# Block loads on one or two DMA queues, and the order of small steps on GpSimd, in a bucketed attention and channel-mix kernel

## The chip, the cores and the metric

The kernel runs on one core of a Trainium2 chip. The metric is the device time of one execution in microseconds; the time of a kernel is the median over its runs. The engines are named as in the profile: PE (TensorE matmuls), PEld (its weight loads), DVE (VectorE), ACT (ScalarE), POOL (GpSimd) and SP (SyncE). SP, ACT and POOL also issue DMAs; a name with a q (SPq, ACTq) is such an engine's sequencer.

## The reference

Two layers in sequence. The first is attention with a mask by hash bucket (B = 4, H = 8, S = 768, D = 64; q, k, v in float32):

```python
q_bits = (np.einsum('bhsd,dk->bhsk', q, proj) > 0)      # proj: 64 x 6
k_bits = (np.einsum('bhsd,dk->bhsk', k, proj) > 0)
q_bucket, k_bucket = sum(bits * 2 ** arange(6))         # 64 buckets
scores = (q @ k.T) / 8, -1e9 where the buckets differ
attn = softmax(scores) @ v                              # denominator + 1e-9
```

Its output, 8 heads of 64 side by side, is x (4 x 768 x 512) of an RWKV channel mix:

```python
xk = mu_k * x + (1 - mu_k) * x_prev                     # x_prev: x shifted by one token
xr = mu_r * x + (1 - mu_r) * x_prev
k = np.maximum(xk @ w_k, 0)                             # w_k: 512 x 1024
out = sigmoid(xr @ w_r) * ((k * k) @ w_v)               # w_r: 512 x 512, w_v: 1024 x 512
```

## The kernel before

**Pairs and slots.** The 32 heads are worked on as 16 pairs, four pairs to a batch. A pair has 12 slots, for two heads of six chunks of 128 keys. The main loop runs over the slots G of all pairs; n is the pair and s the slot in it. `score` (L444, L451) issues two matmuls of 70 contraction rows and one exponential on ACT, which writes the tile pt. The 70 rows are 64 of the head and 6 bucket bits, as plus and minus a half: the bias and the scale of the exponential make the scores of unequal buckets vanish. `pv` (L462, L471) follows two slots later with the product with v; the denominator is a column of ones in va. After a pair `turn_out` (L496 to L502) transposes its output into xt, and shifts columns into a copy of the last token of the block before (a memset and a copy, L501 and L502; on GpSimd except for the last pair of a batch).

**How a pair gets ready.** Pairs 0 to 2 come by `load_qk` and are transposed on PE. Pairs from 3 on come by `load_blocks`: eight DMAs of 176 KB (side q or k, head j, half h), each of which writes 32 partitions from 32 * (2j + h). All eight are on SP. `turn_blocks` transposes 32 x 32 blocks on DVE (tq and tk, L347) and casts them on GpSimd into the rows aq and ak (L357, L359). `bits_blocks` multiplies with the projection on PE (bb, L373), one slot later takes the signs on DVE (sg, L383), and sends them by eight SP DMAs of 4.5 KB into rows 64 to 69 of aq and ak (L388). For pairs 1 and 2 that is `bits` (L401, L405, L411). All this runs ahead: in pair n, `load_blocks(n + 3)` and `load_v(n + 2)` are called at slot 1 (5 in pair 0, 3 in pair 1), `turn_blocks(n + 2)` at slots 7 and 8 of pairs 1 to 3 (6 and 7 in the first pair of a batch from pair 4 on, 4 and 5 in the others), and `bits_blocks(n + 2)` at slot 11 (10 from pair 4 on). blk has two buffers, vf three, and the sets of aq, ak and va are three.

**Values.** `values(n, j)` makes the bfloat16 tile va of head j and the sum vs of its rows on GpSimd (L428, L432 to L434) from vf.

**FFN.** From slot 5 of pair 4 on a queue of FFN items of the batch before is worked off between the slots, so many as a credit per slot allows: kp = xk w_k (L546, relu on ACT L569 or DVE L571, square on DVE L579), rp = xr w_r (tanh on ACT L588), vp = k2 w_v (os on DVE L611, stored by SP L615). The weights come by DMAs of GpSimd in the slots that the table `weights` gives.

**The order** on every engine is that of the program, written out by hand. `later(k, fn)` puts a function off to the start of a slot: `run_due()` runs, at the start of slot G, everything whose time is up, so that k = 0 and k = 1 within a slot both mean the next slot.

Of the kernel before, what the change touches and what calls it, by code (L numbers as in the profile page):

```python
# [31 lines left out]
def kernel(  # L32
# [13 lines left out]
    nc = tc.nc  # L46
# [8 lines left out]
    NPB = H // 2  # L55
    NPAIRS = B * NPB
# [121 lines left out]
    def fast():  # L178
        with ExitStack() as fx:
# [29 lines left out]
            for s in range(NSET):  # L209
                d = {}  # L210
# [6 lines left out]
            for s in range(NSET):  # L217
                d = []
# [16 lines left out]
            def later(k, fn):  # L235
                due.append((clock[0] + k, len(due), fn))

            def run_due():
                ready = sorted(x[:2] for x in due if x[0] <= clock[0])
                for key in ready:  # L240
                    fn = next(x for x in due if x[:2] == key)
                    due.remove(fn)
                    fn[2]()
# [19 lines left out]
                        )  # L263

            NTOK = S // 32

            def load_blocks(n):


                b, t = divmod(n, NPB)  # L270
                xb = blkp.tile([P, 2, NTOK, D], FP32, name=f"blk{n}", tag="blk")
                blks[n] = xb
                run = NC_ * D - 32
                for side, i, src in SIDES:
                    for j in range(2):
                        rows = src[b, 2 * t + j].rearrange("(w i c) d -> i w (c d)", w=4, i=32)
                        for h in range(2):
                            r0 = 32 * (2 * j + h)
                            nc.sync.dma_start(  # L279
                                out=xb[r0 : r0 + 32, i].rearrange("p (w c) d -> p w (c d)", w=4)[  # L280
                                    :, :, 0:run
                                ],
                                in_=rows[:, :, 32 * h : 32 * h + run],
                            )

            def load_v(n):
                b, t = divmod(n, NPB)
                vf = vfp.tile([P, 2, S // 2], FP32, name=f"vf{n}", tag="vf")
                nc.sync.dma_start(
                    out=vf, in_=v[b, 2 * t : 2 * t + 2].rearrange("j (p c) d -> p j (c d)", c=NC_)  # L290
                )
                vfs[n] = vf


            def norm(n, i):
# [8 lines left out]
                else:  # L304

                    nc.scalar.activation(
                        junk.rearrange("p (u d) -> p u d", u=NTOK),
                        blks[n][:, i, :, 0:32],
# [107 lines left out]
            def values(n, j):  # L416
                vf = vfs[n][:, j, :]
                va, vs = vsets[n % NSET][j]
                if n < NSET:
                    nc.gpsimd.memset(va[:, :, D : D + 1], 1.0)  # L420
                    nc.gpsimd.memset(vs[:, D : D + 1], float(NC_))
                if n < NKEEP:
                    nc.gpsimd.tensor_copy(
                        va[:, :, 0:D].rearrange("p (e c) d -> p e c d", e=2),
                        vf.rearrange("p (c e d) -> p e c d", e=2, d=D),
                    )
                else:
                    nc.gpsimd.tensor_copy(  # L428
                        va[:, :, 0:D], vf.rearrange("p (c d) -> p c d", d=D)
                    )  # L430
                s3 = sgp.tile([P, 3 * D], FP32, name=f"s3{n}_{j}", tag="s3")
                nc.gpsimd.tensor_add(s3, vf[:, 0 : 3 * D], vf[:, 3 * D : 6 * D])  # L432
                nc.gpsimd.tensor_add(s3[:, 0:D], s3[:, 0:D], s3[:, D : 2 * D])
                nc.gpsimd.tensor_add(vs[:, 0:D], s3[:, 0:D], s3[:, 2 * D : 3 * D])  # L434
                vas[n, j], vss[n, j] = va, vs
# [223 lines left out]
            def load_w(which, c0, nch):  # L659
                dst, src = {"k": (wk_sb, moe_w_k), "r": (wr_sb, moe_w_r), "v": (wv_sb, moe_w_v)}[  # L660
                    which
                ]
                nc.gpsimd.dma_start(
                    out=dst[:, c0 : c0 + nch, :],
                    in_=src[c0 * P : (c0 + nch) * P, :].rearrange("(c p) f -> p c f", p=P),
                )
# [11 lines left out]
            for _ in range(22):  # L678
# [6 lines left out]
            turn(0, 1, 1, "D")  # L685
            bits(0, (1,), "C")
            load_v(1)
            nc.sync.dma_start(
                out=mu_rows[0:NDC, :], in_=moe_mu_k.rearrange("(c p) -> c p", p=P)
            )  # L690
            nc.sync.dma_start(
                out=mu_rows[NDC : 2 * NDC, :], in_=moe_mu_r.rearrange("(c p) -> c p", p=P)
# [9 lines left out]
                0: {2: ("k", 0, 2)},  # L702
                2: {0: ("k", 2, 2)},
                3: {4: ("r", 0, 2), 8: ("r", 2, 2)},
                4: {11: ("v", 0, 4)},
                5: {10: ("v", 4, 4)},
            }
            LAG = 2
            MIXSLOT = 6
# [11 lines left out]
            for G in range(nslots + LAG):  # L721
                clock[0] = G
                n, s = divmod(G, 12)
                live = G < nslots
                run_due()

                if live and s == (5 if n == 0 else 3 if n == 1 else 1):
                    if n + 2 < NPAIRS:
                        load_v(n + 2)
                    if n + 3 < NPAIRS:  # L730
                        load_blocks(n + 3)
                w = weights.get(n, {}).get(s)
                if w:
                    load_w(*w)
                old = chunks[G - LAG] if G >= LAG else None
                first = old is not None and old[2] == 0
                if live:
                    score(*chunks[G])
                if old and not first:
                    pv(*old, oo_bank(*old[:2]))  # L740
                rate = 25.9 / (NPB * 12 + (3 if n >= NPAIRS - NPB else 0))
                ffn(rate / 2)
                mb = misc_bank(n, s)
                if live:
                    if n == 0:
                        if s in (0, 1):
                            turn(1, s, 1, "BD"[s])
                    if n == 1 and s == 0:
                        mups = bank(mb, [P, 2 * NDC], FP32, "mups")
                        nc.tensor.transpose(mups, mu_rows, ident32[0 : 2 * NDC, 0 : 2 * NDC])  # L750
                        nc.vector.tensor_copy(mu_sb, mups)
                    if s == (3 if n == 0 else 1) and n + 1 < NKEEP:
                        bits(n + 1, (0, 1), mb)
                    if s == (11 if n < NPB else 10) and NKEEP <= n + 2 < NPAIRS:
                        bits_blocks(n + 2, mb if n < NPB else "A")
                    if s == 3 and n >= 1:
                        turn_out(n - 1, mb)
                    if n >= NPB:
                        if s == 4 and n % NPB == 0:
                            mix((n - 1) // NPB, (n - 1) % NPB, 0)  # L760

                        if s in (8, 9) and n % NPB:
                            mix((n - 1) // NPB, (n - 1) % NPB, 0, [(0,), (1, 2)][s - 8])
                    ms = (5, 6, 11)
                    if s in ms and 1 <= n < NPB:
                        mix(0, n - 1, 0, [ms.index(s)])

                    xs = [NPB * 12 + x for x in (5, 10, 11, 12)]
                    if G in xs:
                        mix(0, xs.index(G), 1)  # L770
                    if n > NPB and s == (10 if n % NPB else 5):
                        mix((n - 1) // NPB, (n - 1) % NPB, 1)
                    if s in (5, 7, 9, 11) and n + 2 < NKEEP:
                        x = (s - 5) // 2
                        turn(n + 2, x % 2, x // 2, mb)
                    ts = (7, 8) if n < NPB else (6, 7) if n % NPB == 0 else (4, 5)
                    if s in ts and NKEEP <= n + 2 < NPAIRS:
                        turn_blocks(n + 2, ts.index(s))
                    vs_ = (6, 10) if n == 0 else (0, 2)
                    if s in vs_ and n + 1 < NPAIRS:  # L780
                        values(n + 1, vs_.index(s))
                    if s - 2 in ts and NKEEP <= n + 2 < NKEEP + NLARGE:
                        largest(n + 2, ts.index(s - 2))
                    if s in (8, 10) and NKEEP + NLARGE <= n + 2 < NPAIRS:
                        norm(n + 2, (s - 8) // 2)
                ffn(rate / 2)
                if old and first:
                    pv(*old, oo_bank(*old[:2]))
                if live and n >= NPB and n % NPB == 0 and s == MIXSLOT - 1:
                    queue.extend(ffn_items(n // NPB - 1))  # L790
# [218 lines left out]
```

## Time and profile before

| | us |
|---|---|
| median of 3 runs | 275.18 (274.89 to 275.69) |
| the profiled execution | 277.73 |
| its span | 275.9 |
| PE busy | 250.1 (91%) |
| ACT busy | 210.3 (76%) |
| DVE busy | 179.7 (65%) |
| POOL busy | 123.3 (45%) |
| mean granted PE clock | 0.971 of full speed |

The page gives the busy time of each engine over the span, then the span in 40 slices of 6.9 us (a digit is the busy share in tenths), the DMA queues, the chain of work that ended last, and the costliest groups of instructions. The trace also answers for a stretch of time: rows of an engine's instructions with the idle time before each group in brackets, waits, the chain of waits, and windows. Start times are microseconds from the start of the span. The SP queue's 24,744 packets carry 32.32 MB; the DMAs of GpSimd carry 4.19 MB.

### The profile page before, as it was taken

Reading aid. Unit: us, or ns where it says so; the run is one execution under the profiler, and the core shown is the slowest. Engines: PE = TensorE matmul, PEld = TensorE weight load, DVE = VectorE, ACT = ScalarE, POOL = GpSimd, SP = SyncE. Lnnn points to the kernel's source line nnn. Section 1 sums busy time; section 2 is a strip of 40 time slices with the busy share of each in tenths; the row PEclk is TensorE's granted clock in tenths of the full one; section 3 lists DMA queues with packets and bytes.
Section 4 is the critical chain, followed back from the end, with each engine's and each line's share of the span. In section 5 each row is a group of like instructions: output and inputs, shape, how many; then the busy total and the mean of one; then the engine's idle time right before and its main releaser. Section 6 shows DMA issues by size and latency. Waiting matters only on the chain.

```text
span 275.9 us, 6536 instructions
## 1 busy us (share of the span) xinstructions
PE 250.1 (91%) x2377; PEld 149.1 (54%) x2407; DVE 179.7 (65%) x369; ACT 210.3 (76%) x306; POOL 123.3 (45%) x246
## 2 busy tenths in 40 slices
PE   7899786989995999999999999998999999899970
PEld 5466452656552564656565656564656665455440
DVE  3765546497876676677779696758596646776340
ACT  2199785699995999797999998988999988086100
POOL 5886593667674355550748093815583000000000
PEclk9999999599997999999999999999999999999995
DMA  7457695979594947393949091968720002220140
GB/s 249 155 115 180 125 227 125 240 156 222 128 222 128 217 118 161 103 239 106 246 150 209 7 234 39 216 172 208 181 62 7 2 2 76 78 76 0 46 169 30
DMA packets 27769, 37.42 MB, mean 136 GB/s; under 512 B 3400, under 2 KB 23952, under 8 KB 27728
## 3 DMA queue, kind: packets, MB, share of 16 engines
q1 hardware_dynamic: 24744, 32.32, 46.4%
q0 software_dynamic: 2592, 4.19, 7.6%
q8 instruction: 21, 0.34, 0.5%
q10 hardware_dynamic: 392, 0.40, 0.4%
q14 instruction: 20, 0.16, 0.2%
HBM read 32.64 MB, written 6.29 MB: 141 GB/s over the span
## 4 chain that ended last, share of the span: by engine, by line
PE 57%; DMA 18%; ACT 8%; SPq 6%; DVE 5%; issue 3%; POOL 0%; ACTq 0%; DVEq 0%; POOLq 0%
PE sc L444 14%; PE vp L546 13%; PE kp L546 10%; DMA blk<-in_k_dram 8%; PE oo L471 7%; ACT pt L451 6%; PE rp L546 5%; DMA vf<-in_v_dram 5%; PE bb L373 3%; SPq L279 2%; SPq L411 2%; PE ot L496 2%; DMA blk<-in_q_dram 1%; PE oo L462 1%; DMA aq<-sg 1%
## 5 line engine op out<-in xcount | busy, mean ns | idle before, releaser
L451 ACT ACTIVATE pt<-sc,expb 128x768 bf16<-128x768 f32 x192 | 166.5, 910 | 33.5 <-PE sc L444 31.2
L444 PE MATMUL sc<-aq,ak 70*128 70x384 bf16 x384 | 96.4, 332 | 4.3 <-ACT pt L451 1.1
L471 PEld LDWEIGHTS <-pt 128*128 128x128 bf16 x1152 | 61.9, 99 | 28.2 <-issue 2.5
L471 PE MATMUL oo<-va,pt 128*128 128x65 bf16 x1152 | 67.7, 195 | 0.0
L546 PE MATMUL kp<-xk,wk_sb 128*128 128x384 bf16 x256 | 55.7, 325 | 2.6 <-DVE kr L571 1.1
L444 PEld LDWEIGHTS <-ak 70*128 70x128 bf16 x384 | 35.1, 99 | 34.6 <-issue 12.7
L546 PE MATMUL vp<-wv_sb,k 128*128 128x512 bf16 (+1 forms) x188 | 48.8, 370 | 0.4
L357 POOL CAST aq<-tq 64x768 bf16<-64x768 f32 x26 | 21.4, 823 | 33.3 <-DVE tq L347 21.1
L579 DVE TENSOR_TENSOR k<-kr 128x384 bf16<-128x384 bf16 x64 | 27.3, 442 | 3.4 <-ACT kr L569 3.0
L546 PEld LDWEIGHTS <-wk_sb 128*128 128x128 bf16 x256 | 21.7, 97 | 14.1 <-issue 4.0
L546 PE MATMUL rp<-wr_sb,xr 128*128 128x512 bf16 x78 | 25.4, 391 | 3.5 <-DVE kr L571 2.8
L359 POOL TENSOR_SCALAR ak<-tk 64x768 bf16<-64x768 f32 x26 | 22.3, 857 | 8.5 <-DVE tk L347 6.7
L569 ACT ACTIVATE kr<-kp 128x384 bf16<-128x384 f32 x36 | 18.1, 502 | 9.3 <-PE kp L546 9.2
L546 PEld LDWEIGHTS <-k 128*128 128x128 bf16 x200 | 16.9, 97 | 12.8 <-issue 2.5
L611 DVE SCALAR_TENSOR_TENSOR os<-th,vp 128x512 f32<-128x512 bf16 (+1 forms) x25 | 16.5, 662 | 9.6 <-PE vp L546 7.5
L502 POOL COPY xt<-xt 128x127 bf16<-128x127 bf16 x12 | 3.5, 294 | 42.8 <-DVE xt L497 42.8
L432 POOL TENSOR_TENSOR s<-vf 128x192 f32<-128x192 f32 x32 | 21.3, 665 | 0.0
L571 DVE TENSOR_SCALAR kr<-kp 128x384 bf16<-128x384 f32 x28 | 15.4, 550 | 8.4 <-PE kp L546 8.2
L497 DVE COPY xt<-ot 128x768 bf16<-128x768 bf16 x16 | 8.9, 556 | 18.2 <-PE ot L496 18.2
L482 DVE RECIPROCAL rc<-oo 128x6 f32<-128x6 f32 x32 | 6.1, 191 | 21.6 <-PE oo L471 21.6
L428 POOL CAST va<-vf 128x384 bf16<-128x384 f32 x26 | 15.1, 582 | 8.0 <-DMA vf<-in_v_dram 7.6
L483 DVE TENSOR_TENSOR ob<-oo,rc 128x384 bf16<-128x384 f32 x32 | 17.8, 557 | 1.1
(79 smaller groups left out, 279.8 us busy)
## 6 DMA issues: line engine op xcount, KB each, us to landing
blk<-in_q_dram SPq DMA_DIRECT2D x52, 176.0 KB
blk<-in_k_dram SPq DMA_DIRECT2D x52, 176.0 KB
vf<-in_v_dram SPq DMA_DIRECT2D x16, 384.0 KB
out_dram<-os SPq DMA_DIRECT2D x23, 256.0 KB
aq<-sg SPq DMA_DIRECT2D x64, 4.5 KB
wk_sb<-in_moe_w_k_dram POOLq DMA_DIRECT2D x2, 512.0 KB, 7.3
wv_sb<-in_moe_w_v_dram POOLq DMA_DIRECT2D x2, 512.0 KB, 10.4
ak<-sg SPq DMA_DIRECT2D x62, 4.5 KB
```

What stands on the lines that cost most here:

```text
L357: eng.tensor_copy(dst, src)
L359: eng.tensor_scalar(out=dst, in0=src, scalar1=ALPHA, scalar2=1.0, op0=ALU.mult, op1=ALU.mult,)
L432: nc.gpsimd.tensor_add(s3, vf[:, 0 : 3 * D], vf[:, 3 * D : 6 * D])
L444: nc.tensor.matmul(sc[:, sp, 0:HALF], au["k", j][:, jc * P : (jc + 1) * P], au["q", j][:, sp * HALF : (sp + 1) * HALF], start=True, stop=True,
L451: nc.scalar.activation(pt.rearrange("p (s q) -> p s q", s=2), sc[:, :, 0:HALF], AF.Exp, bias=expb, scale=SCALE,)
L471: nc.tensor.matmul(oo[:, ic, :], pts[n, j, jc][:, ic * P : (ic + 1) * P], vas[n, j][:, jc, :], start=False, stop=(jc == NC_ - 1 and ic == ...
L483: nc.vector.tensor_tensor(out=obs[n][:, :, j * D : (j + 1) * D], in0=oo[:, :, 0:D], in1=rc.to_broadcast([P, NC_, D]), op=ALU.mult,)
L546: nc.tensor.matmul(box["t"], lhs(), rhs(), start=(i == 0), stop=(i == len(mms) - 1))
L569: nc.scalar.activation(kr, kp, AF.Relu, scale=HALFROOT)
L571: nc.vector.tensor_scalar(out=kr, in0=kp, scalar1=0.0, scalar2=HALFROOT, op0=ALU.max, op1=ALU.mult,)
L579: lambda: nc.vector.tensor_tensor(out=k2, in0=kr, in1=kr, op=ALU.mult),
L611: nc.vector.scalar_tensor_tensor(out=os_, in0=mx["th", b, c][:, ms], scalar=1.0, in1=vp, op0=ALU.add, op1=ALU.mult,)
```

## The change

It has four parts.

1. `load_blocks` for pairs 3 to 8 (NTWO = 9): the loads of head j = 0, partitions 0 to 63, are issued on SP at once, those of j = 1, partitions 64 to 127, on ACT's queue, by `later(0)` to `later(3)`: two at the start of the next slot and one at the start of each of the two slots after. The order of the loops over h and j is exchanged, for pairs from 9 on too, which stay on SP.
2. `load_v(2)` is issued in the preamble, after `load_v(1)` and ahead of the mu rows; in the loop `load_v(n + 2)` begins with pair 1.
3. The first half of w_v is loaded from slot 2 of pair 5 rather than slot 11 of pair 4.
4. In pairs before the fifth, `values(n + 1, 0)` is called at slot 4 (6 in pair 0, as before) and `values(n, 1)` at slot 0 of its own pair; from the fifth pair on `values(n + 1, j)` stand at slots 0 and 2 as before, with `values(4, 1)` at slot 0 of pair 4. In pairs 1 to 3 the shift of columns in `turn_out` (slot 3) thus precedes `values(n + 1, ·)` on GpSimd.

```diff
+            NTWO = 9
...
+                k = 0
                 for side, i, src in SIDES:
-                    for j in range(2):
-                        rows = src[b, 2 * t + j].rearrange("(w i c) d -> i w (c d)", w=4, i=32)
-                        for h in range(2):
+                    for h in range(2):
+                        for j in range(2):
+                            rows = src[b, 2 * t + j].rearrange("(w i c) d -> i w (c d)", w=4, i=32)
                             r0 = 32 * (2 * j + h)
-                            nc.sync.dma_start(
-                                out=xb[r0 : r0 + 32, i].rearrange("p (w c) d -> p w (c d)", w=4)[
-                                    :, :, 0:run
-                                ],
-                                in_=rows[:, :, 32 * h : 32 * h + run],
-                            )
+
+                            def load(eng, r0=r0, i=i, h=h, rows=rows):
+                                eng.dma_start(
+                                    out=xb[r0 : r0 + 32, i].rearrange(
+                                        "p (w c) d -> p w (c d)", w=4
+                                    )[:, :, 0:run],
+                                    in_=rows[:, :, 32 * h : 32 * h + run],
+                                )
+
+                            if j and n < NTWO:
+                                later(k, lambda load=load: load(nc.scalar))
+                                k += 1
+                            else:
+                                load(nc.sync)
...
             load_v(1)
+            load_v(2)
...
-                4: {11: ("v", 0, 4)},
-                5: {10: ("v", 4, 4)},
+                5: {2: ("v", 0, 4), 10: ("v", 4, 4)},
...
-                    if n + 2 < NPAIRS:
+                    if 1 <= n < NPAIRS - 2:
                         load_v(n + 2)
...
-                    vs_ = (6, 10) if n == 0 else (0, 2)
-                    if s in vs_ and n + 1 < NPAIRS:
-                        values(n + 1, vs_.index(s))
+                    if n < NPB:
+                        if s == (6 if n == 0 else 4):
+                            values(n + 1, 0)
+                        if n and s == 0:
+                            values(n, 1)
+                    else:
+                        if s == 0 and n == NPB:
+                            values(n, 1)
+                        if s in (0, 2) and n + 1 < NPAIRS:
+                            values(n + 1, s // 2)
```

## The prediction

> **What bounds the kernel now.** I read the page's 40 slices first. TensorE (PE) is full except in slices 5, 7 and 13, each 6.9 us long, and ScalarE (ACT) has its holes in the same places:
>
> ```profile
> PE   7899786989995999999999999998999999899970
> ACT  2199785699995999797999998988999988086100
> ```
>
> The first pairs, to about 61 us, are a stage without FFN work, in which ACT's exponentials set the pace: 12 slots of 0.79 us, 9.5 us for a pair. From slot 5 of pair 4 on PE is the bound, since FFN matmuls fill what the scores leave. So I look for what stopped both, in ACT's own rows (start, duration, engine and line, operation, and in brackets the idle time before and who ended it):
>
> ```profile
> 16.37 8.22 ACT L451 ACTIVATE pt<-sc,expb 128x768 bf16<-128x768 f32 x10 [0.43 <-PE sc L444]
> 25.07 8.02 ACT L451 ACTIVATE pt<-sc,expb 128x768 bf16<-128x768 f32 x10 [0.47 <-PE sc L444]
> 35.36 9.61 ACT L451 ACTIVATE pt<-sc,expb 128x768 bf16<-128x768 f32 x12 [2.27 <-PE sc L444]
> 49.07 2.84 ACT L451 ACTIVATE pt<-sc,expb 128x768 bf16<-128x768 f32 x3 [4.10 <-PE sc L444]
> 87.18 0.90 ACT L451 ACTIVATE pt<-sc,expb 128x768 bf16<-128x768 f32 x1 [3.26 <-PE sc L444]
> ```
>
> Three stalls: 2.27 before 35.36, 4.10 before 49.07, 3.26 before 87.18. What lies in front of them the chain of waits says (start, duration, what):
>
> ```profile
> 26.10 6.61 DMA blk<-in_k_dram
> 36.83 5.83 DMA blk<-in_k_dram
> 42.68 3.68 DMA ak<-sg
> 46.36 0.97 DVE tk L347
> 75.13 9.13 DMA blk<-in_k_dram
> 84.39 0.98 DVE tk L347
> ```
>
> All three are block loads that land late and hold the DVE transpose. The windows of 3.41 us (window, length, busy time of PE, PEld, DVE, ACT, POOL, then granted PE clock, DMA share, GB/s) show the second price, the clock afterwards:
>
> ```profile
> 44.75:48.16 3.41, 1.03 (x8) 0.17 (x8) 1.82 (x3) 0.22 (x1) 1.87 (x3) 0.99 0.07 18
> 48.16:51.57 3.41, 3.41 (x29) 2.16 (x27) 2.61 (x5) 2.36 (x3) 1.24 (x3) 0.50 0.93 248
> 82.26:85.67 3.41, 0.79 (x10) 0.44 (x9) 1.28 (x2) 1.56 (x3) 0.50 (x2) 1.00 0.09 18
> ```
>
> The clock is 0.50 from 48.16 to 54.98 and from 85.67 to 89.08. Five exponentials from 49.07 need 4.84 to 53.91 instead of four times 0.79 = 3.16: 1.7 us lost to each such stretch. Pairs take (from first exponential to first exponential) 10.2, 12.5, 13.7, 11.9, 13.7 and 19.1 us for pairs 0 to 5, 14.0 to 14.7 after that.
>
> **The change part by part.** *Half of the blocks to ACT's queue.* SP loses 24 issues of 0.43 to 0.46 us; ACT's sequencer gains 24. Bandwidth is no gain: the loads of one pair land one each 0.83 us (26.93, 27.79, 28.61 and so on), 176 KB in 0.83 us or 212 GB/s at a DMA share over 1, while vf, with 128 partitions, runs at 345 to 409 GB/s. Whether halves on two queues go side by side or in turn no row shows: between nothing (8 x 0.83 = 6.6 us for a pair) and half (3.3 us). I take nothing; either way the data would then land 4 us or more before its transposes.
>
> The Trainium skill, "DMA: Bandwidth & Descriptors", section "Rules for kernel authors", speaks against it: spreading over issuing engines brings no bandwidth, and two transfers to disjoint halves of the partitions serialize; only issue time is saved. "SBUF — State Buffer", section "Can I just issue two DMAs to hit both halves?", gives +6% for two at once. By that figure a pair's load would be 6.3 us, an estimate; the sum stays as it is.
>
> The gain is that ACT's half no longer stands behind SP's eight small DMAs of the bucket bits (0.66 to 0.70 us each). They and the blocks hold each other up in the queue; SP's waits (who waited, for whom, total us, times, longest) say so:
>
> ```profile
> SPq L388 <- DMA blk<-in_q_dram: 6.1, 13, 1.2
> SPq L388 <- DMA blk<-in_k_dram: 5.3, 7, 2.3
> ```
>
> In pair 4 the eight bits issue from 63.68 to 71.20 and the blocks of pair 7 start only at 71.75, ten us behind their slot.
>
> The price is new waits on ACT. In the program as built every DMA of SP and ACT waits on one of eight counters, shared by both queues, until the DMA before it on that counter has landed. For the new ACT loads these are, in pair 0, a mu row and bits 3 and 6 of pair 1; in pairs 1 to 5 the 1st, 4th and 6th bits DMA of the pair two on, issued in the same pair. Behind a waiting load stand ACT's exponentials, and PE waits for those (two score tiles).
>
> *Pair 0.* Bits 1 to 8 issue on SP from 16.55 at 0.70; the first landed in 1.8 us (18.35), the third and sixth only at 22.26 and 22.84, for GpSimd's first half of w_k (issued 16.80, landed 22.1) was in the way. So the exponential of slot 8 starts not at 19.57 but after 22.84, two issues of 0.45 and a semaphore: 23.9. That is +4.3. Without the hold, bit 6 would land at 16.55 + 5 x 0.70 + 1.8 = 21.9 and slot 8 start at 22.4: +2.8. I take 4.3, since GpSimd's order there does not change.
>
> *Pairs 1 to 3.* With t the first exponential of the pair, sg (the bits) is ready at t + 0.8 (36.55 against 35.36, 50.0 against 49.07), bit 6 issues 5 x 0.70 later, lands 1.8 later and the load issues: t + 6.6. It stands ahead of the exponential of slot 4, and eight are left: 6.6 + 8 x 0.79 = 12.9. In pair 1 sg comes at t + 2.3 and the load stands ahead of slot 6: 8.15 + 6 x 0.79 = 12.9. Against 12.5, 13.7 and 11.9 that is +0.4, -0.8, +1.0. The old stalls at 35 and 49 are in the old periods, so they are gained and paid back here.
>
> *Pair 4.* Slot 4 moves from t + 3.2 (64.15) to t + 6.6: 3.4 later, and the FFN starts after it. PE had holes here and may catch up a part; between 0 and 3.4, taken 2.5, as the matmuls freed are few before slot 5.
>
> *Pair 5.* It is 4.7 us over its neighbours' mean (19.1 against 14.4): the stall at 83 to 86 and a half-clock window. ACT's half of the pair's blocks now issues near its slot, SP's half is four issues rather than eight, and the 4.7 go; late next are the load's own issues on ACT and its waits, under PE's work, 0.5. Net -4.2.
>
> *Clock.* Each stop of ACT for 2.5 to 3.4 us leaves PE two slots of work and then nothing. A PE hole of 2.4 us cost the clock in one place (44.97 to 47.37), and PE busy for 2.35 of 3.40 at 31.10 did not. For five such stops I take one half-clock stretch more than now and a little, 2.0; bounds 0 and four stretches, 6.8.
>
> *The rest, priced at nothing.* vf of pair 2 goes out 8 us earlier, SP's 0.45 us falling in its idle 15.52 to 16.55; uncovered, its 384 KB would hold the first bits DMA by 1.0. wv's first half issues 3 slots later, at about 77 instead of 73.08, landing by 87 to 91; its first matmul is at 105.9, so 15 us cover it. On GpSimd a half of the values is 0.58 + 0.67 + 2 x 0.32 = 1.9 us; the shift of columns (0.10 + 0.29) now goes ahead of it. The second half at slot 0 of its own pair is read first in slot 8, 6 us on; if GpSimd were behind by more, up to 1.9 per pair. GpSimd is busy 45% of the span, so nothing.
>
> **Sum.** 4.3 + 0.4 - 0.8 + 1.0 + 2.5 - 4.2 + 2.0 = +5.2 us. The profiled execution took 277.73 (span 275.9), 2.5 over the median of 275.18; I add the difference to the median: 280.4.
>
> **The rivals.** *Faster: ACT hardly waits.* If the bits have landed by the time ACT gets to its loads, under one exponential (0.8 us) of wait a pair, the stalls are gained: 2.3 + 4.1 + 1.7 + 4.7 = 12.8. Paid are 2.8 in pair 0 and 0.3 in each of pairs 1 to 4 (two issues in one slot, 0.9 against 0.79), 4.0. Since bits and casts still have to pass, I count 10 of the 12.8: -6, 269. For it: bits on an idle queue take 1.8 us, and SP is no longer held by blocks. Against: five issues at 0.70 before the sixth bit, which no faster transfer shortens. It decides at a wait of about 0.8 us a pair.
>
> *Even.* If pair 0 costs 2.8, PE catches up all of pair 4, and no clock window is added, the sum is 5.2 - 1.5 - 2.5 - 2.0 = -0.8: 274.4.
>
> *Slower still: every stop costs the clock.* Four stretches of 1.7, in place of 2.0, make 285.2. For it: the stops are as long as the two that did so. Against: the 31.10 window.
>
> *It does nothing.* If both queues drained as one and ACT's loads were late anyway, the three stalls would stand: 275.2. Against it: ACT's waits come from the program.
>
> **How the numbers follow.** Forecast 0.42, faster rival 0.22, even 0.14, slower still 0.20, nothing 0.02. Below 268.5 lies a third of the faster case, above 286 a third of the slower still: 0.14 outside. A measurement of this kernel tells 0.3%, 0.8 us, from no change. Even gives 0.05 faster, 0.05 same and 0.04 slower; so faster is 0.22 + 0.05 = 0.27, same 0.05 + 0.02 = 0.07, slower 0.42 + 0.20 + 0.04 = 0.66. As both signs hold much, the likeliest case by itself: 277 to 284.
>
> **What would show it.** Right: in ACT's rows a gap of 3 to 4 us near 20 us, ended by ACT's own queue with a wait for aq or ak from sg, and gaps of 2 to 3 us near slot 4 of pairs 2 to 4; first exponentials of pairs 1 to 4 12.9 apart; no hole in PE near 83. Wrong: pairs 1 to 4 at 10 to 11 us with ACT's loads issued between exponentials without idle time (the faster rival); a pair 5 still at 19 us (then the wv load, not SP's queue, held the blocks); or clock 0.50 in more than two stretches (the slower one).

## The result, and the profile after

The changed kernel took 299.17 us (median of 295.76, 299.10, 299.24 and one execution of 1385 us, which is left out of all ratios here and below, as slow executions are) against 275.44 for the kernel before, measured with it: a ratio of 1.0821, 95% interval 1.0728 to 1.0914. The profiled execution took 299.24, span 297.4. The direction was as forecast, the size was not: +24 us where +5 was expected, and above the range. Pairs 6 to 14 take 128.4 us in both profiled executions, and what follows them was 2.2 us shorter in the changed kernel's; the loss is in pairs 0 to 5:

| from first exponential to first exponential, us | pair 0 | 1 | 2 | 3 | 4 | 5 | sum |
|---|---|---|---|---|---|---|---|
| before | 10.2 | 12.5 | 13.7 | 11.9 | 13.7 | 19.1 | 81.1 |
| forecast, without its 2.0 for the clock | 14.5 | 12.9 | 12.9 | 12.9 | 16.2 | 14.9 | 84.3 |
| after | 16.9 | 17.4 | 16.9 | 15.4 | 17.3 | 20.8 | 104.7 |

The page's slices of the span (297.4 us, 7.4 us a slice) have more holes than before, and the clock (third row) is low from slice 4 to slice 12 without a break, and again in slice 15:

```profile
PE   7877967895969599999999999999899999989991
ACT  1246573876759469998989999988899998629400
PEclk9985677568779969999999999999999999999997
```

ACT's waits (who waited, for whom, total us, times, longest) name the new cause. In the kernel before ACT waited for no DMA:

```profile
ACT pt L462 <- DMA ak<-sg: 14.0, 5, 3.8
...
ACT pt L462 <- DMA blk<-in_q_dram: 3.3, 1, 3.3
...
ACT pt L462 <- DMA mu_rows<-in_moe_mu_r_dram: 1.8, 1, 1.8
```

19.1 us of exponentials held up behind a load, most often until a DMA of bucket bits (ak<-sg, 4.5 KB) had landed. ACT's rows show where, in pairs 0 and 1 (ACTq rows are the loads' issues):

```profile
19.40 0.32 ACTq L283 DMA_DIRECT2D blk<-in_q_dram  x1
19.82 0.90 ACT L462 ACTIVATE pt<-sc,expb 128x768 bf16<-128x768 f32 x1 [1.77 <-DMA mu_rows<-in_moe_mu_r_dram]
22.99 0.32 ACTq L283 DMA_DIRECT2D blk<-in_k_dram  x1
23.42 0.90 ACT L462 ACTIVATE pt<-sc,expb 128x768 bf16<-128x768 f32 x1 [2.70 <-DMA ak<-sg]
...
38.53 0.32 ACTq L283 DMA_DIRECT2D blk<-in_k_dram  x1
38.95 0.90 ACT L462 ACTIVATE pt<-sc,expb 128x768 bf16<-128x768 f32 x1 [2.50 <-DMA ak<-sg]
```

The load issues late, the exponential comes 0.4 us behind it, and its bracket has the wait. The windows that follow (the columns of the windows of before) show what the forecast underrated:

```profile
17.44:20.86 3.42, 1.66 (x20) 1.15 (x19) 2.62 (x6) 1.51 (x2) 2.67 (x9) 0.98 1.04 228
20.86:24.27 3.41, 1.37 (x9) 0.74 (x9) 0.00 (x0) 0.85 (x2) 0.29 (x1) 0.50 0.54 125
24.27:27.68 3.41, 3.31 (x23) 2.23 (x23) 0.91 (x2) 2.49 (x4) 0.69 (x1) 0.50 1.04 263
27.68:31.09 3.41, 3.41 (x31) 2.46 (x33) 1.13 (x3) 2.19 (x4) 1.60 (x5) 0.50 0.23 41
31.09:34.51 3.42, 3.42 (x24) 1.33 (x25) 1.31 (x3) 1.55 (x2) 0.88 (x4) 0.52 0.00 0
34.51:37.92 3.41, 2.38 (x37) 1.69 (x34) 2.09 (x3) 1.80 (x2) 2.06 (x7) 1.00 0.45 117
```

One stop of ACT, and PE runs at half clock for four windows, although it is busy throughout the last three. In the 34 windows from 14 to 130 us the clock is at 0.50 to 0.52 in 15; in the kernel before it was in 3.

### The profile page after: what moved, and what is told of

It is laid out like the page before. It is cut to its first block, busy times and chain, and to the rows that moved or that the text cites. A ratio compares the mean times of both kernels' runs of the same rounds, so it can differ in the third digit from the quotient of the medians.

```text
span 297.4 us, 6569 instructions
## 1 busy us (share of the span) xinstructions
PE 265.5 (89%) x2407; PEld 155.7 (52%) x2407; DVE 181.7 (61%) x369; ACT 213.3 (72%) x306; POOL 126.1 (42%) x246
## 4 chain that ended last, share of the span: by engine, by line
PE 70%; DMA 12%; ACT 7%; DVE 4%; SPq 2%; issue 2%; ACTq 1%; DVEq 0%
PE sc L455 20%; PE vp L557 13%; PE kp L557 11%; PE oo L482 10%; PE rp L557 6%; DMA ak<-sg 6%; ACT pt L462 5%; PE bb L384 4%; PE oo L473 2%; PE bb L412 1%; DMA blk<-in_k_dram 1%; DMA aq<-sg 1%; PE ot L507 1%; DMA blk<-in_q_dram 1%; DMA projp<-in_proj_dram 1%
## 5 line engine op out<-in xcount | busy, mean ns | idle before, releaser
L462 ACT ACTIVATE pt<-sc,expb 128x768 bf16<-128x768 f32 x192 | 169.7, 908 | 53.0 <-PE sc L455 29.9
L455 PE MATMUL sc<-aq,ak 70*128 70x384 bf16 x384 | 105.3, 359 | 17.4 <-ACT pt L462 16.2
L482 PEld LDWEIGHTS <-pt 128*128 128x128 bf16 x1152 | 67.3, 104 | 33.5 <-issue 11.2
L482 PE MATMUL oo<-va,pt 128*128 128x65 bf16 x1152 | 72.7, 203 | 0.0
L455 PEld LDWEIGHTS <-ak 70*128 70x128 bf16 x384 | 36.0, 103 | 51.4 <-issue 30.4
L557 PE MATMUL kp<-xk,wk_sb 128*128 128x384 bf16 x256 | 56.9, 331 | 2.2 <-DVE kr L582 1.1
L557 PE MATMUL vp<-wv_sb,k 128*128 128x512 bf16 (+1 forms) x200 | 51.8, 371 | 0.0
L368 POOL CAST aq<-tq 64x768 bf16<-64x768 f32 x26 | 21.4, 823 | 41.0 <-PE sc L455 16.2
L590 DVE TENSOR_TENSOR k<-kr 128x384 bf16<-128x384 bf16 x64 | 26.8, 433 | 11.5 <-ACT kr L580 11.1
L557 PE MATMUL rp<-wr_sb,xr 128*128 128x512 bf16 x96 | 29.9, 389 | 3.5 <-ACT kr L580 3.5
L557 PEld LDWEIGHTS <-wk_sb 128*128 128x128 bf16 x256 | 22.1, 99 | 14.6 <-issue 4.5
L557 PEld LDWEIGHTS <-k 128*128 128x128 bf16 x200 | 16.9, 97 | 12.8 <-issue 2.5
L443 POOL TENSOR_TENSOR s<-vf 128x192 f32<-128x192 f32 x32 | 22.9, 716 | 0.0
L622 DVE SCALAR_TENSOR_TENSOR os<-th,vp 128x512 f32<-128x512 bf16 (+1 forms) x25 | 16.5, 662 | 8.4 <-PE vp L557 8.4
L582 DVE TENSOR_SCALAR kr<-kp 128x384 bf16<-128x384 f32 x28 | 15.4, 552 | 9.9 <-PE kp L557 9.7
L317 ACT ACTIVATE sq<-blk 128x768 bf16<-128x768 f32 x20 | 17.0, 852 | 0.0
```

The costliest lines, as they stand in the source:

```text
L317: nc.scalar.activation(junk.rearrange("p (u d) -> p u d", u=NTOK), blks[n][:, i, :, 0:32], AF.Square, scale=1.5, accum_out=nrm[:, i, n : n ...
L368: eng.tensor_copy(dst, src)
L455: nc.tensor.matmul(sc[:, sp, 0:HALF], au["k", j][:, jc * P : (jc + 1) * P], au["q", j][:, sp * HALF : (sp + 1) * HALF], start=True, stop=True,
L462: nc.scalar.activation(pt.rearrange("p (s q) -> p s q", s=2), sc[:, :, 0:HALF], AF.Exp, bias=expb, scale=SCALE,)
L482: nc.tensor.matmul(oo[:, ic, :], pts[n, j, jc][:, ic * P : (ic + 1) * P], vas[n, j][:, jc, :], start=False, stop=(jc == NC_ - 1 and ic == ...
L557: nc.tensor.matmul(box["t"], lhs(), rhs(), start=(i == 0), stop=(i == len(mms) - 1))
```

## The experiments

Theory A: ACT stands at its new loads until DMAs on the counters that it shares with SP have landed, PE empties, and the clock halves. The trace of the change has the counters: the DMAs of SP and of ACT complete on the same eight semaphores (100, 102, 104 to 107, 117, 118), those of GpSimd on eight others (109 to 116). B: the loss comes from the other three parts of the change. C: two queues loading at once slow each other. Ratios are to the kernel before, measured in the same job.

**One part each.** The block loads of the change alone, and the change without them:

```diff
e1: kernel before + only part 1 of the change
e2: the change with
-            NTWO = 9
+            NTWO = 0
```

> Only the first part of the change on the kernel before: half of the block loads of pairs 3 to 8 on ACT's queue; vf of pair 2, wv and the values as before. Theory A (ACT's sequencer stands at the new loads until small bits DMAs have landed, PE empties, and the PE clock halves after each such stop): the whole loss is here, 294 to 301 us. Theory B (the loss comes from the order on GpSimd or the earlier vf load, which make the bits of the next pairs late): 272 to 279 us.

> The change with NTWO = 0: all block loads on SP, in the new order of h and j, and the other three parts kept. Theory A: no loss, 270 to 277 us (the stall at 83 us gone with the later wv load, or not). Theory B: 290 us or more.

Measured: 296.78 us (1.0739, 1.0654 to 1.0824) and 272.02 us (0.986, 0.9814 to 0.9905). B falls. The other parts, with the new order of h and j, are a gain of 1.4%, and ACT's half costs 27 us on top of them.

**wv alone.**

```diff
-                4: {11: ("v", 0, 4)},
-                5: {10: ("v", 4, 4)},
+                5: {2: ("v", 0, 4), 10: ("v", 4, 4)},
```

> The kernel before with the wv load alone moved to slot 2 of pair 5. If the wv load held the blocks of pair 7 (stall at 83 us): pair 5 takes 14 to 16 us rather than 19.1, 270 to 272 us. If SP's order held them: 274 us or more.

Measured: 273.69 us (0.9949, 0.9917 to 0.998), between the two expectations; pair 5 decides. In the profiled execution (271.39 us) it took 15.4 us rather than 19.1, and in e2, e7 and e11 below, which have this part too and all loads on SP, 14.3 to 15.0. So moving the wv load away from the blocks of pair 7 is enough, with SP's order as it was. It is not the only way: in e1, where wv stayed, the blocks of pair 7 were all issued by 88.7, before wv at 94.4, and the transposes of pair 5 did not stall. The rest of the gain of e2 was not divided further.

**One pair only.**

```diff
-            NTWO = 9
+            NTWO = 4
```

> The change with NTWO = 4: only the blocks of pair 3, issued in pair 0, are split over SP and ACT; the others stay on SP. Theory A, refined by the runs so far (each stop of ACT costs its length, and then a stretch at half the PE clock in which a slot takes 0.97 us rather than 0.79): pair 0 takes 16 to 17 us, pair 1 11 to 13.5, the rest as with all loads on SP, 276 to 282 us. Theory D (the six pairs' stops do not add up, one of them would have cost nearly all): 288 us or more.

Measured: 277.05 us (1.0036, 0.9993 to 1.0079); by the two ratios 0.018, or some 5 us, over e2 (in another job). In the profiled execution, of 279.25 us, pair 0 took 16.5 us against 10.1 in e2; one exponential waited 4.16 us for a bits DMA. The rest, some 2 us, is pace at half clock. The stops add up: one costs 5 us, six cost 27.

**Other times for ACT's loads.** First by 8 or 9 slots more:

```diff
-                                later(k, lambda load=load: load(nc.scalar))
+                                later(k + (8 if n == 3 else 9), lambda load=load: load(nc.scalar))
```

> The change with ACT's half issued 6 to 8 slots later, when the bits DMAs that the loads wait for have mostly landed; everything else as in the change. Theory A: ACT's idle time before its loads falls from 19 us to under 5 us, the clock stays over 0.96, 266 to 277 us. Theory C (two queues that load blocks at the same time slow each other and the small DMAs down): the transposes of pairs 3 to 8 still wait, 285 us or more.

As run, the loads lay 7 to 9 slots later than in the change, not 6 to 8. Measured: 302.85 us (1.0966, 1.0894 to 1.1037). The expectation failed. ACT's waits were no shorter, since the last loads now came among the next pair's bits, and some waited for a block load. ACT's rows of this kernel:

```profile
28.54 4.51 ACT L462 ACTIVATE pt<-sc,expb 128x768 bf16<-128x768 f32 x5 [1.85 <-DMA blk<-in_q_dram]
...
45.11 1.69 ACT L462 ACTIVATE pt<-sc,expb 128x768 bf16<-128x768 f32 x2 [4.93 <-DMA ak<-sg]
```

Then four slots earlier, ahead of the bits of the pair, on both queues and on SP alone:

```diff
e6 (e7 the same, with all eight loads on nc.sync):
-                    if n + 3 < NPAIRS:
+                    if n + 3 < NPAIRS and not 4 <= n + 3 < NTWO:
                         load_blocks(n + 3)
+                if live and s == (9 if n < NPB else 11) and 4 <= n + 4 < NTWO:
+                    load_blocks(n + 4)
...
-                            if j and n < NTWO:
-                                later(k, lambda load=load: load(nc.scalar))
+                            if j and 4 <= n < NTWO:
+                                later((1, 1, 2, 2)[k], lambda load=load: load(nc.scalar))
```

> The change, but the blocks of pairs 4 to 8 are called for four slots earlier (slot 9 of the pair before; slot 11 for pair 8), ahead of the next pair's bits DMAs, half of them on ACT's queue in the two slots after; pair 3's all on SP. The DMAs that ACT's loads then wait for on the shared counters landed a pair ago. Theory A (ACT's queue harms only by the waits on bits DMAs in flight): no ACT wait over 1 us before a load, clock over 0.98, 260 to 268 us. Theory C (two queues loading at once slow each other or the small DMAs): no better than with all loads on SP, 270 us or more.

> As the early kernel, but all eight loads of a pair on SP. If the time of the issue and not the queue is what counts, within 3 us of the early kernel with two queues. If SP's eight issues (3.7 us) ahead of the bits delay these: 2 to 5 us slower than it.

Measured: 291.11 us (1.0532, 1.0448 to 1.0616) and 272.15 us (0.9854, 0.9786 to 0.9922). Theory A as it stood expected 260 to 268 and missed, as did both cases for e7, and for C this looked good. But the rows show what had been left out: the counters hold both ways. SP's bits DMAs (first row, from SP's rows) now waited 5 us for one of ACT's loads (of 37.05, on the same semaphore, 100), and later one of ACT's loads for vf (two rows of ACT):

```profile
34.27 6.25 SPq L422 DMA_DIRECT2D ak<-sg  x2
```

```profile
64.35 6.13 ACTq L283 DMA_DIRECT2D blk<-in_k_dram  x2
70.58 1.69 ACT L462 ACTIVATE pt<-sc,expb 128x768 bf16<-128x768 f32 x2 [5.50 <-DMA vf<-in_v_dram]
```

Two issues that take 1.36 us elsewhere took 6.25. Last, slots in between, chosen pair by pair:

```diff
+            LATE = {3: (8, 8, 8, 8), 4: (6, 6, 7, 7), 5: (8, 8, 9, 9), 6: (8, 8, 9, 9), 7: (7, 7, 8, 8), 8: (6, 6, 7, 7)}
...
-                                later(k, lambda load=load: load(nc.scalar))
+                                later(LATE[n][k], lambda load=load: load(nc.scalar))
```

> The change with ACT's loads at slots 7 to 11 of the pair (13 for pair 3): later than the bits DMAs that they wait for were issued, and earlier than the next pair's, and so between the change and the first late kernel, whose loads fell among the next pair's bits. If only waits on DMAs in flight matter: ACT waits under 1.5 us a pair, 268 to 280 us. If ACT's queue cannot be used for blocks at all: 290 us or more.

Measured: 282.83 us (1.0278, 1.0226 to 1.033): between the two cases expected, the best of the placements on ACT of more than one pair's loads, and still 11 us over e2. No wait for bits is left, but others have come in, as ACT's waits say:

```profile
ACT pt L463 <- DMA vf<-in_v_dram: 5.6, 3, 3.4
ACT pt L463 <- DVE tk L359: 2.5, 2, 1.3
ACT pt L463 <- DMA blk<-in_q_dram: 2.4, 1, 2.4
```

**Another queue.** This parts A from C: two queues at the same slots, but counters of their own.

```diff
-                                later(k, lambda load=load: load(nc.scalar))
+                                later(k, lambda load=load: load(nc.gpsimd))
```

> The change with the second half of the block loads on GpSimd's queue in the place of ACT's, at the same slots. GpSimd's DMAs have eight counters of their own, on which only its earlier loads stand, all long landed. Theory A (the wait on the counters that SP and ACT share, not the splitting over two queues, stops the kernel): no ACT wait for a DMA, 264 to 275 us, with GpSimd's issues of about 0.8 us each hidden. Theory C (splitting itself, two queues on the same engines, is the harm): 285 us or more.

Measured: 269.01 us (0.9795, 0.973 to 0.9861), as A expected. ACT waited for no DMA. C falls, and with it the thought that halves on two queues are harmful in themselves. (This run changes two things, the counters and the engine that would stand at them; that it was the counters at which ACT stood is read from ACT's waits and the semaphores.) ACT's rows still hold one stall, before 48.27, and the chain of waits has its cause:

```profile
35.28 9.62 ACT L462 ACTIVATE pt<-sc,expb 128x768 bf16<-128x768 f32 x12 [0.45 <-PE sc L455]
48.27 9.62 ACT L462 ACTIVATE pt<-sc,expb 128x768 bf16<-128x768 f32 x12 [3.37 <-PE sc L455]
```

```profile
39.42 4.25 DMA aq<-sg
...
44.03 0.98 DVE tq L358
```

A bits DMA took 4.25 us, while w_k's second half and the blocks were under way, and a DVE transpose behind it.

**What a stop costs.** First, PE kept busy during ACT's waits by matmuls on constants, 18 of 384 columns at seven places, then 6 to 18 at eight places:

```diff
e5 (e10 with 6 to 18 of them, at eight places):
+                if (n, s) in ((0, 8), (0, 9), (1, 7), (2, 4), (3, 5), (4, 5), (5, 4)):
+                    fill = bank(misc_bank(n, s), [P, 3, P], FP32, f"fill{G}")
+                    for _ in range(18):
+                        nc.tensor.matmul(fill, epsm, epsm[:, None, :].to_broadcast([P, 3, P]),
+                                         start=True, stop=True)
```

> The change, with 18 matmuls of 384 columns on constants (some 3 us) put on PE ahead of the seven scores at which PE stands still while ACT waits, so that PE stays busy; ACT's waits stay. Theory A: ACT's waits are as long as before, the clock is over 0.95, and 279 to 287 us are left: the difference to 299 is what the clock costs. If the clock cost little, the time stays at 297 or more.

> The change with filling matmuls on PE again, now 6 to 18 at eight places, fitted to the lengths of PE's holes, so that they do not outlast them. ACT's waits for bits stay, about 19 us. If the clock after the stops is worth 10 to 14 us: clock over 0.96 and 284 to 291 us. If the stops alone make the loss: 296 us or more with the clock up.

Measured: 298.18 us (1.084, 1.0774 to 1.0905) and 297.4 us (1.0821, 1.0743 to 1.0899). Taken as totals these speak for stops alone; but the fills are no clean test. Where they fit, the time came down: in e10 the first exponential of pair 3 came at 57.57 against 63.84, with the clock at 1.00 up to 51.6, as in these windows, and in two of ACT's rows, from pair 1:

```profile
20.86:24.27 3.41, 2.31 (x16) 1.27 (x13) 0.00 (x0) 0.45 (x1) 0.24 (x1) 1.00 0.47 114
24.27:27.68 3.41, 2.79 (x34) 2.12 (x34) 1.08 (x3) 3.41 (x5) 0.69 (x1) 1.00 0.89 233
...
35.17 0.90 ACT L462 ACTIVATE pt<-sc,expb 128x768 bf16<-128x768 f32 x1 [1.86 <-DMA ak<-sg]
35.97 4.85 ACT L462 ACTIVATE pt<-sc,expb 128x768 bf16<-128x768 f32 x6
```

Pair 1 is the clean comparison. In e10 the clock is at 1.00 all through it, two exponentials come 0.76 and 1.97 us late behind loads, and it takes 13.37 us: the 10.64 of e9 and these two, nothing more. In the change it waited 2.50 us for a load and took 17.37: 4.2 us more than its wait accounts for, with a mean clock of 0.70.

In pair 5 the fill came after the hole and made it longer (25.1 us rather than 20.8). And ACT's waits grew, to 20.3 us for bits alone: presumably because a load that waits for a DMA with a time of its own waits longer when all ahead of it runs faster; this was not tested.

So the stop was made without a DMA: in e9, spare activations on ACT ahead of slot 4 in pairs 1 to 4, three or five of them.

```diff
+                if s == 4 and 1 <= n <= 4:
+                    for x in range(3):                      # e15: range(5)
+                        stop = sqp.tile([P, S], BF16, name=f"stop{n}_{x}", tag="sq")
+                        nc.scalar.activation(
+                            stop, nats[0][:, 0].rearrange("p j f -> p (j f)"), AF.Square
+                        )
```

> The kernel with half of the blocks on GpSimd's queue (no ACT wait for a DMA), with three spare activations over 768 elements (some 0.8 us each, 2.4 us in all) put on ACT ahead of the exponential of slot 4 in pairs 1 to 4: a stop of known length without any DMA. If a stop costs its length: 269 + 4 x 2.4 = 278 to 280 us, clock as before. If PE's clock falls after each: 282 to 288 us, clock under 0.96.

> As with the short stops, with five spare activations, some 4.0 us a stop. Length alone: 269 + 4 x 4.0 = 284 to 286 us. With the clock falling after each stop: 290 to 298 us, clock under 0.95.

Measured: 282.89 us (1.0275, 1.0228 to 1.0323) and 290.62 us (1.0528, 1.0474 to 1.0581), clocks 0.945 and 0.931. One row of ACT's with a stop, and the windows of the short stops, over the first two:

```profile
26.40 2.59 ACT L751 ACTIVATE stop<-qk 128x768 bf16<-128x768 f32 x3
...
27.69:31.10 3.41, 1.27 (x10) 0.82 (x10) 0.46 (x1) 3.38 (x5) 3.06 (x9) 0.84 0.65 141
31.10:34.51 3.41, 3.41 (x28) 2.10 (x26) 2.68 (x5) 2.88 (x4) 0.86 (x2) 0.50 0.98 272
...
41.34:44.75 3.41, 0.81 (x10) 0.50 (x8) 1.52 (x2) 3.35 (x5) 3.33 (x8) 0.84 1.06 236
44.75:48.17 3.42, 3.42 (x28) 2.06 (x26) 1.68 (x4) 3.01 (x4) 0.49 (x2) 0.50 1.04 221
```

The clock fell after each of the four. Pair 1, which has no other stall, prices a stop: exponentials 3 and 4 lie 3.28 apart rather than 0.79, a stop of 2.5 us, and the pair takes 15.07 us against 10.64 in e9, 4.4 more: 1.9 us for the clock. With five activations it is 4.2 us, and 17.41 - 10.64 = 6.8: 2.5 for the clock. The totals give less: 13.9 and 21.6 us over e9, of which the four stops are 10.0 and 17.0, so 1.0 to 1.2 a stop. But e9's profiled execution has the stall in pair 2, and its pairs 0 and 5 take 11.5 and 16.1 us, against 10.1 and 14.6 with the short stops.

**Towards a better kernel.** All on SP, with pairs 5 to 8 early only, and the GpSimd version with two places mended:

```diff
e11: e7 with
-... not 4 <= n + 3 < NTWO:          ... and 4 <= n + 4 < NTWO:
+... not 5 <= n + 3 < NTWO:          ... and 5 <= n + 4 < NTWO:
e12: e9 with
-                            if j and n < NTWO:
+                            if j and 4 <= n < NTWO:
-                2: {0: ("k", 2, 2)},
+                2: {9: ("k", 2, 2)},
```

> All block loads on SP; pair 3 and 4 at the times of the change, pairs 5 to 8 four slots earlier (slot 9 of the pair before), the other parts of the change kept. If the stalls left in pairs 2 and 3 are blocks that start too late behind the bits: pair 1 near 10.6, pairs 2 and 3 near 10.1 to 11 us, 264 to 269 us. If the early loads push the bits back instead (as in pair 1 of the early kernel on SP): 270 us or more.

> As the kernel with half of the blocks on GpSimd's queue, with two places mended that its profile shows: pair 3's blocks stay on SP (GpSimd's issues in pair 0 delayed its casts there, pair 0 took 11.5 us rather than 10.1), and the second half of w_k is loaded at slot 9 of pair 2 rather than slot 0 (it ran beside the small bits DMAs, one of which took 4.25 us and ended the idle time before a transpose at 44 us). Expected if both readings are right: pair 0 10.1 us, pair 2 10 to 11 us, 264 to 267 us. If the blocks themselves hold the bits back: 268 us or more.

e11: 274.03 us (0.9983, 0.9936 to 1.003), the worse of its two cases; pair 2 took 17.3 us, since the last of pair 4's blocks landed 8.47 us after its issue and a bits DMA took 4.06 us behind them. e12: 268.73 us (0.9782, 0.9745 to 0.9819), faster than both kernels, but not the 264 to 267 expected. Pair 0 came back to 10.06 us and pair 2 to 11.29, as read from e9, though a bits DMA there still took 3.61 us. For pair 0 the reading is not shown: with the short stops, where its loads are those of e9, it took 10.06 us too. Pair 3 took 12.4 rather than 10.7, with three of GpSimd's own load issues (1.68 us) in its chain of waits. The median is one with e9's.

## Why the prediction was right or wrong

**The new waits: right in place and nearly in sum, the sum in part by luck.** The exponential of slot 8 in pair 0 was put at 23.9 and started at 24.22. The terms of pairs 0 to 4 imply some 18 us of waits on ACT (4.3, then about 3.4 in each of four pairs, 0.5 in pair 5); 19.1 were measured. But pairs 1 to 4 waited 2.5 to 3.3 each, 10.8 instead of 13.6, one to two slots ahead of the place forecast, and pair 5 waited 3.8: two errors that nearly cancel. e1, e2 and e9 show that the waits of ACT's loads are the cause of the loss.

**The clock: wrong, and the step that failed.** "One half-clock stretch more than now and a little, 2.0" was set against a row in which PE was busy for 2.35 of 3.40 us without a fall, at 31.10. That window has no hole of PE over 0.52 us, as PE's row of the kernel before shows:

```profile
32.75 0.83 PE L373 MATMUL bb<-tq,projp 128*32 128x384 f32 x2 [0.52 <-DVE tq L347]
```

The two stalls that did empty PE for long there, 2.38 us at 45 and 2.81 at 83, both brought the clock down, and the new stops are like those two. The windows (of the grid above) ahead of the falls in the changed kernel have PE busy for 0.67 to 1.66 of 3.41, like the rows that did fall, and the stops of all six pairs brought the clock down. ACT's waits replaced 9.6 us of old idle time (2.27 + 4.10 + 3.26), 9.5 net of 23.6; the other 14.1 are pace. The stops without a DMA give 1.9 to 2.5 each in pair 1, 11 to 15 for six (by their totals, 6 to 7), and the pair 1 of the change against that of e10 gives 4.2 for a pair. The term that was set at 2.0 measures about 14, by subtraction; that the clock makes the most of it rests on these pairs. The case "slower still" had the mechanism, but four stretches of 1.7, 6.8, was still half: 1.7 was read from five exponentials of a stretch that goes on through the pair, and a half-clocked pair starts the next one's bits late. Pair 1's sg came 3.6 us after its first exponential, not 2.3.

**Pair 5: wrong.** -4.2 was booked since ACT's half would no longer stand behind SP's; +1.7 came. e8 shows that moving the wv load alone brings 3.7 of these us, and e1 that ACT's half alone parts the blocks from wv too. They were gained, but in pair 5 a load still waited 3.76 us for bits, where 0.5 was priced as hidden under PE's work, and PE emptied and lost its clock there too. Work on PE hid none of ACT's wait here: the next matmul in its order needed ACT's result.

**Pair 4**: +2.5 forecast, +3.6 measured. **Pair 0**: +4.3 against +6.7, of which 2 are pace at half clock.

**The faster rival** has by luck the number of another kernel: its 269 is what e9 took, where ACT does not wait, but where other terms stand, such as a stall of 3.37 us. **The parts priced at nothing** (vf, values) did no harm, taken together: e2 with all three parts gains 1.4%. wv, priced at nothing, is a gain in pair 5 (e8).

## What to carry to other kernels

Before a DMA is moved to another engine's queue, list the DMAs that it must wait for in the built program, and what is queued behind it there: a 0.4 us issue can hold an engine for as long as an unrelated transfer takes. Price a stop of the engine that feeds PE as its length and, on top, what PE loses at half clock until it recovers; here that was 1.9 us on a stop of 2.5 and 2.5 on one of 4.2, in the one pair where it could be read alone. To learn whether a queue or a wait does harm, use a queue with other counters; a test that fills the hole moves the wait.

## What the runs showed of the hardware

PE holes shorter than a window of 3.41 us brought the clock down: 2.60 us, in all four places of the short stops, with PE busy for 0.81 to 2.01 of 3.41 us in the window. Shorter ones are not decided by their length: in e12, after the start, two of 1.40 and 1.72 us passed without a fall; in pair 0 of the change one of 1.64 us (19.13 to 20.77) did not, and in e9 the clock fell at 45.2 with no hole over 1.02 us in the window before. Nor does the busy share of the window decide: in e10 the clock held after 1.81 of 3.41 us (from 22.00) and fell after 2.45 (from 49.31).

The Trainium skill, "TensorE: Matmul & The Clock Gate", section "Why this matters for your kernels", asks for no idle gaps over some 3 us; here 2.60 us was too long already.

The stretches at half clock lasted one to four windows, although PE was busy for 3.41 of 3.41 us in most of these. In the change the stretches that began at 20.7 and 51.4 us ended with a window in which the projection matmuls (bb) ran; whether these ended it was not tried.

A DMA of 4.5 KB that took 1.8 us once (the first of pair 1 in the kernel before, 16.55 to 18.35) took 3.6 to 5.0 us beside block or weight loads (4.96 in the chain of the change, 4.25 in e9, 3.61 in e12).
